# First block's gated unit by rows on centred x, its result turned by DMA

## Chip, cores, metric

One core of one Trainium2 chip. The metric is the device time of one execution in microseconds (us), lower is better. "The kernel before" and "the changed kernel" are the two versions compared.

## The reference, cut to what matters

```python
x = A_x                                   # (1, 2048, 640) bf16
xn = layernorm(x)                         # (x - mean) / sqrt(var + 1e-5), by rows
s = attention(xn, k_cache, v_cache, wq, wo)   # 32 heads, last 512 keys
g = silu((sigmoid(xn @ w_gate) * (xn @ w_up)) @ w_down)   # 640 -> 1536 -> 640
return x + s * g
```

The change is in `sigmoid(xn @ w_gate) * (xn @ w_up)` for the first 512 of the 2048 rows ("block 0"), at the start of the program. Since the layer norm's root is one number per row, `(xc * rstd) @ w = rstd * (xc @ w)` with `xc = x - mean`: with rows on the partitions the root can be applied after the matmul. "By rows" below means a result with the rows of x on the partitions and F along the free dimension, "by columns" one with F on the partitions; "turned" means transposed.

## The kernel before

Block 0, first four of twelve 128-column pieces of F, tile by tile of 128 rows, result with F on the partitions:

```python
def stats_end(t):                         # t < 2: root on ScalarE, reciprocal on VectorE
    nc.vector.bn_aggr(mv[:], ln[t][:])
    nc.scalar.activation(rstd[:], mv[:, 1:2], AF.Sqrt, bias=eps_t[:], scale=1.0)
    nc.vector.reciprocal(rstd[:], rstd[:])
    # (t >= 2: add on VectorE, pow -0.5 on GpSimd)

def normal(t, parts): ...                 # xn = (x - mean) * rstd, VectorE
def turn_pe(t, c0, c1, k): ...            # xn transposed on TensorE, copied to xnT[:, 0] by ScalarE

def tile_half(t, half, c0=0, c1=NCD):
    w = (wg_sb, wu_sb)[half]
    for c in range(c0, c1):
        for f in range(4):
            nc.tensor.matmul(bank[t % 3][:, half, f * P:(f + 1) * P],
                             lhsT=w[:, c, f * P:(f + 1) * P],
                             rhs=xnT[:, 0, c, t * P:(t + 1) * P], ...)   # 128 columns
# ... cut: sigmoid on ScalarE, product on VectorE, straight into hT[0]
for f in range(4, NF):                    # the other eight pieces: 512 columns
    gated(0, f, k, norm_piece(1, f - 4))  # norm_piece: layer norm of block 1, turned by DMA
for b in range(1, NB):
    for f in range(2):
        gated(b, f, k)
    for q in range(TQ):
        down(b - 1, q, k)                 # reads hT[b - 1]
    # ... cut
```

TensorE begins with 24 matmuls on dummy data ("dummies") while x is loaded.

The softmax here doesn't subtract the row's maximum and nothing guards it: scores larger than these inputs give would overflow.

## Time and profile before

| | before |
|---|---|
| time, median (range) of 4 runs | 922.59 us (922.28 to 923.13) |
| span of the profiled run | 920.3 us |
| TensorE busy | 915.1 us, 99% |
| first matmul of block 1 | 33.58 us |
| first down-projection | 37.89 us |

How to read it: TensorE is the bound, and its stream of matmuls runs without holes from about 9 us on, so whatever moves the start of a late matmul moves the end by as much. I use two such marks: the first matmul of block 1, which shows what the head cost, and the first down-projection, which is the first to read block 0's result. The profile's own lines are in the prediction.

### The profile page before, as it was taken

What the parts mean: (1) busy time and instruction counts of PE and PEld (TensorE: products, weight loads), DVE (VectorE), ACT (ScalarE), POOL (GpSimd) and SP (SyncE); (2) the same over time, 40 slices, a digit from 0 to 9 for tenths busy, and PEclk for the clock granted to TensorE, in tenths of its full rate; (3) what the DMA queues carried; (4) which work ended last, traced back from release to release, by engine and by line L of the source; (5) the groups of instructions that cost most, each with busy time, mean ns of one, the idle gap of its engine ahead of it and who ended that gap; (6) DMA issues with size and microseconds to landing.
All of it is one profiled execution on the core that took longest, in us unless ns stands there. A gap on an engine that the chain in (4) does not pass through costs nothing.

```text
span 920.3 us, 25202 instructions
## 1 busy us (share of the span) xinstructions
PE 915.1 (99%) x11460; PEld 628.5 (68%) x11460; DVE 491.7 (53%) x983; ACT 303.4 (33%) x336; POOL 133.6 (15%) x157
## 2 busy tenths in 40 slices
PE   9999999999999999999999999999999999999998
PEld 7445455466868686867676777777776767686875
DVE  5452522545646464645555555545564646464677
ACT  4222222255142424232333333242424151515150
POOL 1000100011002000200120011001100111065643
PEclk9999999999999999999999999999999999999999
DMA  9310330115434534342425162616251624263535
GB/s 320 81 30 1 89 86 1 43 62 88 78 63 106 86 57 83 93 99 42 98 81 111 36 104 79 113 28 112 65 109 43 116 61 94 63 113 111 90 81 136
DMA packets 163147, 77.14 MB, mean 84 GB/s; under 512 B 140992, under 2 KB 158608, under 8 KB 163040
## 3 DMA queue, kind: packets, MB, share of 16 engines
q1 hardware_dynamic: 155680, 53.62, 29.5%
q0 software_dynamic: 5808, 20.52, 7.9%
q8 instruction: 89, 1.46, 0.7%
q10 hardware_dynamic: 1552, 1.39, 0.5%
q14 instruction: 18, 0.15, 0.0%
HBM read 39.45 MB, written 2.62 MB: 46 GB/s over the span
## 4 chain that ended last, share of the span: by engine, by line
PE 99%; DVE 0%; ACT 0%; DVEq 0%; issue 0%
PE bank L504 22%; PE bank L433 21%; PE bank L455 19%; PE bank L415 18%; PE bank L242 10%; PE bank L254 6%; PE bank L381 1%; PE bank L287 1%; PE bank L190 0%; PE bank L539 0%; DVE o_sb L485 0%; DVE gate L490 0%; PE bank L226 0%; ACT xnT L228 0%; DVEq L641 0%
## 5 line engine op out<-in xcount | busy, mean ns | idle before, releaser
L419 ACT ACTIVATE E<-bank 128x1024 bf16<-128x1024 f32 x256 | 255.5, 1023 | 456.4 <-PE bank L415 456.3
L433 PE MATMUL bank<-xnT,wq_sb 64*128 64x512 bf16 x1800 | 226.4, 376 | 0.0
L504 PE MATMUL bank<-wo_sb,oT 64*128 64x320 bf16 x2688 | 205.2, 296 | 0.0
L415 PE MATMUL bank<-qT,kT 64*128 64x512 bf16 x1536 | 200.7, 376 | 0.0
L455 PE MATMUL bank<-vbuf,E 64*128 64x193 bf16 x4096 | 195.3, 243 | 0.0
L455 PEld LDWEIGHTS <-E 64*128 64x128 bf16 x4096 | 178.8, 94 | 10.2 <-issue 0.3
L504 PEld LDWEIGHTS <-oT 64*128 64x128 bf16 (+1 forms) x2892 | 163.2, 94 | 30.8 <-issue 0.5
L440 DVE CAST qT<-bank 128x1024 bf16<-128x1024 f32 x90 | 110.2, 1225 | 128.5 <-PE bank L433 128.5
L433 PEld LDWEIGHTS <-wq_sb 64*128 64x128 bf16 x1800 | 105.9, 100 | 87.2 <-issue 0.4
L415 PEld LDWEIGHTS <-kT 64*128 64x128 bf16 x1536 | 88.1, 94 | 73.5
L468 DVE TENSOR_TENSOR o_st<-bank,rden 128x768 bf16<-128x768 f32 x128 | 122.5, 957 | 4.4
L519 DVE TENSOR_TENSOR acc<-bank,acc 128x640 f32<-128x640 f32 x96 | 79.0, 823 | 20.2 <-PE bank L504 20.2
L118 POOL DMA_DIRECT2D vbuf<-in_A_v_cache_dram x28 | 21.1, 753 | 313.9 <-PE bank L455 310.9
L438 DVE COPY seen<-bank 128x2 f32<-128x2 f32 x90 | 14.3, 159 | 79.1 <-PE bank L433 79.1
L467 DVE RECIPROCAL rden<-bank 128x4 f32<-128x4 f32 x128 | 23.4, 183 | 60.6 <-PE bank L455 59.5
L242 PE MATMUL bank<-xnT,wg_sb 128*128 128x512 bf16 x220 | 54.7, 379 | 0.0
L242 PE MATMUL bank<-xnT,wu_sb 128*128 128x512 bf16 x220 | 54.7, 379 | 0.0
L248 DVE TENSOR_TENSOR hT<-bank,sig 128x512 bf16<-128x512 f32 x44 | 30.3, 689 | 42.1 <-ACT sig L245 42.1
L254 PE MATMUL bank<-wd_sb,hT 128*128 128x512 bf16 (+1 forms) x384 | 52.8, 299 | 0.0
L245 ACT ACTIVATE sig<-bank 128x512 bf16<-128x512 f32 x44 | 26.3, 597 | 68.4 <-PE bank L242 65.3
L254 PEld LDWEIGHTS <-hT 128*128 128x128 bf16 x384 | 29.7, 98 | 23.1
L242 PEld LDWEIGHTS <-wu_sb 128*128 128x128 bf16 x220 | 21.5, 98 | 26.0
(55 smaller groups left out, 367.5 us busy)
## 6 DMA issues: line engine op xcount, KB each, us to landing
wo_sb<-in_A_wo_dram SPq DMA_DIRECT2D x7, 960.0 KB, 5.5
wq_sb<-in_A_wq_dram POOLq DMA_DIRECT2D x7, 960.0 KB, 6.1
k_st<-in_A_k_cache_dram POOLq DMA_DIRECT2D x14, 384.0 KB, 5.3
vbuf<-in_A_v_cache_dram POOLq DMA_DIRECT2D x28, 192.0 KB, 3.4
row<-in_A_x_dram POOLq DMA_DIRECT2D x16, 160.0 KB, 3.1
oT<-o_st SPq DMA_TRANSPOSE x128, 3.5
x_sb<-in_A_x_dram SPq DMA_DIRECT2D x3, 640.0 KB, 10.8
wd_sb<-in_B_w_down_dram SPq DMA_DIRECT2D x1, 1920.0 KB, 14.3
```

What stands on the lines that cost most here:

```text
L242: nc.tensor.matmul(bank[k][:, half, 0:r1 - r0], lhsT=w[:, c, f * P:(f + 1) * P], rhs=xnT[:, b, c, r0:r1], start=(c == 0), stop=(c == NCD - 1))
L245: nc.scalar.activation(sig[:, 0:r1 - r0], bank[k][:, 0, 0:r1 - r0], AF.Sigmoid)
L248: nc.vector.tensor_tensor(hT[b][:, f, r0:r1], bank[k][:, 1, 0:r1 - r0], sig[:, 0:r1 - r0], ALU.mult)
L254: nc.tensor.matmul(wide(k)[:, d0:d1], lhsT=hT[b][:, f, q * P:(q + 1) * P], rhs=wd_sb[:, f, d0:d1], start=(f == 0), stop=(f == NF - 1))
L415: nc.tensor.matmul(bank[k][:, i, :], lhsT=kT[r, pr, j, c * P:(c + 1) * P], rhs=q[r, pr * DJ + j, :], start=(j == 0), stop=(j == DJ - 1))
L419: nc.scalar.activation(E[u, pr][:, c, :, :], bank[k][:], AF.Exp, scale=scale_qk)
L433: nc.tensor.matmul(bank[k][:, half, :], lhsT=wq[r, c, col:col + DJ * (P - 1) + 1:DJ], rhs=xnT[r, b, c, :], start=(c == 0 and not second), ...
L440: nc.vector.tensor_copy(qT[u][:, 2 * m:2 * m + 2, :], bank[k][:])
L455: nc.tensor.matmul(o4[:, q, 0:DH + 1], lhsT=e[r, c, h % 2, q * P:(q + 1) * P], rhs=vbuf[r, h, c, 0:DH + 1], start=(turn == 0 and qq == 0 a ...
L468: nc.vector.tensor_tensor(o_st[u][:, :, h * DH:(h + 1) * DH], o4[:, :, 0:DH], rden[:].to_broadcast([P, TQ, DH]), ALU.mult)
L504: nc.tensor.matmul(res[:, half, :], lhsT=oT[u][r, cc, q * P:(q + 1) * P], rhs=wo[r, cc, half * HD:(half + 1) * HD], start=(turn == 0 and c ...
L519: nc.vector.tensor_tensor(cols(acc[:, t, :]), res, cols(acc[:, t, :]), ALU.add)
```

## The change

Intent: take the root out of the chain that the first matmul waits for, and give block 0 matmuls of 512 columns throughout.

```diff
+        xcT = xnT[:, NB - 1, :, :]              # centred x lies in block 3's place for now
+        h_row = wB.tile([P, TQ, F], BF16, name="h_row")
...
+        def centred(t, parts=((0, 3 * P), (3 * P, D))):
+                nc.vector.tensor_scalar(xc[:, d0:d1], xt[t][:, d0:d1], ln[t][:, 0:1], None,
+                                        op0=ALU.subtract)
...
-                for f in range(FT):
-                    nc.tensor.matmul(bank[t % 3][:, half, f * P:(f + 1) * P],
-                                     lhsT=w[:, c, f * P:(f + 1) * P],
-                                     rhs=xnT[:, 0, c, t * P:(t + 1) * P],
+                nc.tensor.matmul(bank[k][:, half, :], lhsT=xcT[:, c, t * P:(t + 1) * P],
+                                 rhs=w[:, c, fg * FT:(fg + 1) * FT],      # FT = 512
...
+            nc.scalar.activation(sig[:], bank[k][:, 0, :], AF.Sigmoid, scale=rstd[:, 0:1])
+            if between is not None:
+                between()
+            nc.vector.scalar_tensor_tensor(h_row[:, t, fg * FT:(fg + 1) * FT], bank[k][:, 1, :],
+                                           rstd[:, 0:1], sig[:], ALU.mult, ALU.mult)
...
+        steps = [norm_piece(1, i) for i in range(TQ + 1)]
+        steps[TQ:] = [steps[TQ]] + [norm_first(t) for t in range(TQ)]   # xn of block 0, turned by DMA
+        for fg in range(1, F // FT):
+            for t in range(TQ):
+                tile_half(t, fg, k, 0)
+                tile_half(t, fg, k, 1)
+                tile_gated(t, fg, k, steps.pop(0) if steps else None)
+        hT[0] = hpool.tile([P, NF, TB], BF16, name="hT")
+        for t in range(TQ):
+            nc.sync.dma_start_transpose(hT[0][:, :, t * P:(t + 1) * P], h_row[:, t, :])
+        while steps:
+            steps.pop(0)()
```

(All roots now by pow on GpSimd; the table load for the square root goes.) The scaled x of block 0 is still needed, by the attention's queries, so it is normalised later (`norm_first`) and turned by DMA.

More of the change, by code (lines that the diff above doesn't have):

```diff
@@ L182 @@
         load_x(2 * TQ, TQ)
-        nc.scalar.activation(junk[:], eps_t[:], AF.Sqrt)
+        nc.scalar.activation(junk[:], eps_t[:], AF.Sigmoid)
         nc.gpsimd.memset(mhalf[:], -0.5)
@@ L198, in stats_half, with stats_aggr, stats_root, normal @@
             nc.vector.bn_stats(ln[t][:, i, :], xt[t][:, i * (D // 2):(i + 1) * (D // 2)])
-        def stats_end(t):
-            mv = bwork.tile([P, nc.vector.BN_AGGR_DIM], F32, name="mv")
-            rstd = bwork.tile([P, 1], F32, name="rstd")
+        def stats_aggr(t):
+            mv = bwork.tile([P, nc.vector.BN_AGGR_DIM], F32, name="mv0" if t < TQ else "mv")
             nc.vector.bn_aggr(mv[:], ln[t][:])
-            if t < 2:
-                nc.scalar.activation(rstd[:], mv[:, 1:2], AF.Sqrt, bias=eps_t[:], scale=1.0)
-                if t == 0:
-                    stats_half(1, 0)
-                nc.vector.reciprocal(rstd[:], rstd[:])
-            else:
-                nc.vector.tensor_scalar(rstd[:], mv[:, 1:2], eps, None, op0=ALU.add)
-                nc.gpsimd.tensor_tensor(rstd[:], rstd[:], mhalf[:], ALU.pow)
-            ln[t] = mv, rstd
-        def normal(t, parts=((0, D),)):
+            ln[t] = mv
+        def stats_root(t):
+            rstd = bwork.tile([P, 1], F32, name="rstd0" if t < TQ else "rstd")
+            nc.vector.tensor_scalar(rstd[:], ln[t][:, 1:2], eps, None, op0=ALU.add)
+            nc.gpsimd.tensor_tensor(rstd[:], rstd[:], mhalf[:], ALU.pow)
+            ln[t] = ln[t], rstd
+        def normal(t):
             mv, rstd = ln[t]
             xn = xpool.tile([P, D], BF16, name="xn")
+            nc.vector.tensor_scalar(xn[:], xt[t][:], mv[:, 0:1], rstd[:, 0:1],
+                                    op0=ALU.subtract, op1=ALU.mult)
+            xn_t[t] = xn
+        xn_t = {}
+        def centred(t, parts=((0, 3 * P), (3 * P, D))):
+            xc = xpool.tile([P, D], BF16, name="xn")
             for d0, d1 in parts:
-                nc.vector.tensor_scalar(xn[:, d0:d1], xt[t][:, d0:d1], mv[:, 0:1], rstd[:, 0:1],
-                                        op0=ALU.subtract, op1=ALU.mult)
-            ln[t] = xn
+                nc.vector.tensor_scalar(xc[:, d0:d1], xt[t][:, d0:d1], ln[t][:, 0:1], None,
+                                        op0=ALU.subtract)
+            xn_t[t] = xc
         def turn_pe(t, c0=0, c1=NCD, k=3):
@@ L225, in turn_pe @@
             for c in range(c0, c1):
-                nc.tensor.transpose(pT[:, c, :], ln[t][:, c * P:(c + 1) * P], ident[:])
+                nc.tensor.transpose(pT[:, c, :], xn_t[t][:, c * P:(c + 1) * P], ident[:])
             for d0, d1 in ((c0, c1),) if c1 - c0 < NCD else ((0, 3), (3, NCD)):
-                nc.scalar.activation(xnT[:, 0, d0:d1, t * P:(t + 1) * P], pT[:, d0:d1, :], AF.Copy)
+                nc.scalar.activation(xcT[:, d0:d1, t * P:(t + 1) * P], pT[:, d0:d1, :], AF.Copy)
         def turn_dma(t):
             q = t % TQ
-            nc.sync.dma_start_transpose(xnT[:, t // TQ, :, q * P:(q + 1) * P], ln[t][:])
+            nc.sync.dma_start_transpose(xnT[:, t // TQ, :, q * P:(q + 1) * P], xn_t[t][:])
         hT = {}
@@ L270, in step, with tile_half, tile_gated, norm_first @@
                     stats_half(t, 1)
-                    stats_end(t)
+                    stats_aggr(t)
+                    stats_root(t)
             return step if i <= TQ else None
-        FT = 4
-        hT[0] = hpool.tile([P, NF, TB], BF16, name="hT")
-        def tile_half(t, half, c0=0, c1=NCD):
+        FT = 4 * P
+        def tile_half(t, fg, k, half, c0=0, c1=NCD):
             w = (wg_sb, wu_sb)[half]
             for c in range(c0, c1):
-                for f in range(FT):
-                    nc.tensor.matmul(bank[t % 3][:, half, f * P:(f + 1) * P],
-                                     lhsT=w[:, c, f * P:(f + 1) * P],
-                                     rhs=xnT[:, 0, c, t * P:(t + 1) * P],
-                                     start=(c == 0 and f == 0), stop=(c == NCD - 1),
-                                     skip_group_check=True)
-        sigs = {}
-        def tile_sigmoid(t):
-            sigs[t] = bwork.tile([P, TB], BF16, name="sig")
-            nc.scalar.activation(sigs[t][:], bank[t % 3][:, 0, :], AF.Sigmoid)
-        def tile_gated(t):
-            nc.vector.tensor_tensor(
-                hT[0][:, 0:FT, t * P:(t + 1) * P],
-                bank[t % 3][:, 1, :].rearrange("p (f n) -> p f n", f=FT),
-                sigs[t][:].rearrange("p (f n) -> p f n", f=FT), ALU.mult)
+                nc.tensor.matmul(bank[k][:, half, :], lhsT=xcT[:, c, t * P:(t + 1) * P],
+                                 rhs=w[:, c, fg * FT:(fg + 1) * FT],
+                                 start=(c == 0), stop=(c == NCD - 1))
+        def tile_gated(t, fg, k, between=None):
+            rstd = ln[t][1]
+            sig = bwork.tile([P, TB], BF16, name="sig")
+            nc.scalar.activation(sig[:], bank[k][:, 0, :], AF.Sigmoid, scale=rstd[:, 0:1])
[3 more added lines that the diff above has]
+                                           rstd[:, 0:1], sig[:], ALU.mult, ALU.mult)
+        def norm_first(t):
+            def step():
+                normal(t)
+                turn_dma(t)
+            return step
         dummy(18)
@@ L308 @@
         stats_half(0, 1)
-        stats_end(0)
-        normal(0, ((0, P), (P, 3 * P), (3 * P, D)))
+        stats_aggr(0)
+        centred(0, ((0, P), (P, 3 * P), (3 * P, D)))
+        stats_half(1, 0)
+        stats_half(1, 1)
+        stats_aggr(1)
+        centred(1)
+        stats_root(0)
+        stats_root(1)
         turn_pe(0, 0, 1)
         turn_pe(0, 1, 3, 2)
-        tile_half(0, 0, 0, 1)
+        tile_half(0, 0, 0, 0, 0, 1)
         turn_pe(0, 3, NCD, 1)
-        tile_half(0, 0, 1)
@@ L317 @@
-        stats_half(1, 1)
-        stats_end(1)
-        normal(1, ((0, 3 * P), (3 * P, D)))
-        tile_half(0, 1, 0, 2)
+        tile_half(0, 0, 0, 0, 1)
         turn_pe(1, 0, 3)
-        tile_half(0, 1, 2, 3)
         turn_pe(1, 3, NCD, 2)
-        nc.scalar.activation(junk[:], eps_t[:], AF.Sigmoid)
-        tile_half(1, 0)
-        tile_half(0, 1, 3)
-        tile_sigmoid(0)
-        stats_half(2, 0)
-        stats_half(2, 1)
-        stats_end(2)
-        stats_half(3, 0)
-        stats_half(3, 1)
@@ L335 @@
-        normal(2)
-        stats_end(3)
-        tile_gated(0)
-        normal(3)
+        tile_half(0, 0, 0, 1, 0, 3)
+        tile_half(1, 0, 1, 0)
+        tile_half(0, 0, 0, 1, 3)
+        for t in (2, 3):
+            stats_half(t, 0)
+            stats_half(t, 1)
+            stats_aggr(t)
+            centred(t)
+            stats_root(t)
+        tile_gated(0, 0, 0)
         for t in range(1, TQ):
             if t > 1:
-                tile_half(t, 0)
-            tile_half(t, 1, 0, 1)
+                tile_half(t, 0, t % 3, 0)
+            tile_half(t, 0, t % 3, 1, 0, 1)
@@ L343 @@
             if t + 1 < TQ:
                 turn_pe(t + 1)
-            tile_half(t, 1, 1)
-            tile_sigmoid(t)
-            tile_gated(t)
+            tile_half(t, 0, t % 3, 1, 1)
+            tile_gated(t, 0, t % 3)
+        steps = [norm_piece(1, i) for i in range(TQ + 1)]
+        steps[TQ:] = [steps[TQ]] + [norm_first(t) for t in range(TQ)]
         k = 1
-        for f in range(FT, NF):
-            gated(0, f, k, norm_piece(1, f - FT))
-            k = (k + 1) % 4
+        for fg in range(1, F // FT):
[3 more added lines that the diff above has]
+                tile_gated(t, fg, k, steps.pop(0) if steps else None)
+                k = (k + 1) % 4
```

## The prediction

> **What bounds the kernel now.** I read four views of the kernel before, in this order: the page's summary, the chain that ended last over the first 50 us, the timeline of the first 17 us, and the DMA issues with the moving rate of a lone transpose. The summary and the shares of the chain:
>
> ```profile
> span 920.3 us, 25202 instructions
> PE 915.1 (99%) x11460; PEld 628.5 (68%) x11460; DVE 491.7 (53%) x983; ACT 303.4 (33%) x336; POOL 133.6 (15%) x157
> PE 99%; DVE 0%; ACT 0%; DVEq 0%; issue 0%
> ```
>
> TensorE is busy 915.1 of 920.3 us. Nothing that the change does on VectorE, ScalarE or the queues counts unless TensorE stands still for it, or is spared columns or a wait. So the question is small: which columns go, which TensorE waits go, and which come. The chain over the first 50 us says where TensorE now waits inside the region that the change touches:
>
> ```profile
> 1.06 4.21 PE bank L190 x24
> 5.27 0.22 PE bank L226
> 5.49 0.02 issue
> 5.51 0.29 ACT xnT L228
> ...
> 7.86 0.18 PE bank L226 x3
> 8.04 0.02 issue
> 8.07 0.50 ACT xnT L228
> 8.57 0.04 issue
> 8.61 1.95 PE bank L287 x32
> ```
>
> L190 is the warm-up with dummy matmuls, L226 the transposes of x on TensorE, L228 ScalarE's copy of them to SBUF, L287 the first block's 128-column matmuls. There are two holes: about 0.3 us at 5.5 us and 0.5 us at 8.1 us, both ended by a copy of transposed x. The second is there because tile 1 of x is normalised late. The timeline shows why:
>
> ```profile
> 4.10 0.21 DVE L203 BATCH_NORM_AGGREGATE mv<-st 128x2 f32<-128x12 f32 x1
> 4.23 0.44 DVE L198 BATCH_NORM_STATS2 st<-x_sb 128x6 f32<-128x320 bf16 x1
> 4.35 0.29 ACT L205 ACTIVATE rstd<-mv,eps_t 128x1 f32<-128x1 f32 x1 [1.18 <-DVE mv L203]
> 4.67 0.16 DVE L208 RECIPROCAL rstd<-rstd 128x1 f32<-128x1 f32 x1
> 4.87 0.82 DVE L218 TENSOR_SCALAR xn<-x_sb,mv,rstd 128x128 bf16<-128x128 bf16 x3
> ...
> 6.65 0.28 ACT L205 ACTIVATE rstd<-mv,eps_t 128x1 f32<-128x1 f32 x1
> 6.97 0.16 DVE L208 RECIPROCAL rstd<-rstd 128x1 f32<-128x1 f32 x1 [0.63 <-ACT rstd L205]
> 7.17 0.64 DVE L218 TENSOR_SCALAR xn<-x_sb,mv,rstd 128x384 bf16<-128x384 bf16 x2
> ```
>
> The root (ScalarE, then a reciprocal on VectorE) sits between the mean and the normalised x: 0.54 us in tile 0 (4.33 to 4.87), and in tile 1 0.63 us of idle plus the reciprocal. In the same timeline the first 512-column matmul of block 0 starts at 16.31 us, block 1 at 33.58, and the first down-projection of block 0 at 37.89.
>
> **What the Trainium skill says.** "TensorE: Matmul & The Clock Gate", section "Wait — 56ns, not 53.3ns?": a warm matmul of N columns starts N/2.4 GHz plus about 2.5 ns after the one before, 55.6 ns for 128 and 215.7 ns for 512. The trace agrees: twenty of 128 from 11.56 to 12.68 us are 56 ns each, five of 512 from 20.63 to 21.71 are 216 ns. So by rows costs the same per column. "ScalarE: Activation LUTs", section "What ACT_TABLE_LOAD costs": 1283 ns for the load, and about 93 ns more per pointer operand of an ACTIVATE; the trace has loads of 1283 ns, and tiny ACTIVATEs of 203 ns without and 290 ns with a pointer bias. "VectorE: DVE Perf Modes", section "Why PSUM operands drop a tier": an fp32 PSUM source runs at 1x, so I expect the new three-operand product to cost what the old one does, 690 ns for 512; no run shows the new one yet. "DMA: Bandwidth & Descriptors", section "Anatomy of one DMA", puts a fixed 2.0 us on a transfer (measured there on another issue path); here a lone transpose of 160 KB lands in 2.6 us, 1.8 of which is not movement (below).
>
> **The change part by part.**
>
> Matmuls. Removed: 160 of 128 columns (4 tiles x 2 weights x 5 chunks x 4). Added: 40 of 512. Saved: 40 x (4 x 55.6 - 215.7) ns = 0.27 us. The other 80 of block 0 are 512 wide before and after; the 20 transposes of x stay.
>
> Head of the chain. Centring needs only the mean. VectorE: aggregate of tile 0 ends at 4.31, so the three centred parts run 4.33 to 5.15 instead of 4.87 to 5.69. But the dummies occupy TensorE until about 5.14 (six of 64 columns issue by then), so of the 0.54 us only about 0.1 comes through. Then tile 1: two statistics 0.89 (to 6.05), aggregate 0.21 (6.27), two centred parts 0.38 + 0.34, done by 7.0 us where before it was 7.81. TensorE, walked through: transposes from 5.14, first copy to 5.68, matmul c0 at 5.71, c1 and c2 at 6.10, c3 and c4 at about 6.70 to 7.13; transposes of tile 1 to 7.41; three matmuls with the up weights to 8.06, which cover the copies of tile 1 (7.5 to 8.35); so the hole of 0.5 us at 8.1 closes. From there without waits: tile 1's gate 1.08 and tile 0's last two 0.43 to 9.57; tile 1's up with the transposes of tile 2 1.36; tile 2 with the transposes of tile 3 2.44; tile 3 2.16; the end is 15.53. Against 16.31: **0.78 us saved**, 0.27 of it per-matmul cost. The weights allow it: the up weights' halves were issued at 2.13 and 3.17 and land 4.9 and 5.1 us later (7.03, 8.27); they are used at 7.41 and 9.14. The second ScalarE table load (1.28 us at 8.85) goes, but no TensorE wait hung on it.
>
> Eight gated tiles of ten 512-column matmuls take 8 x 2.157 = 17.26 us as before: block 1 starts at 32.8 instead of 33.58. VectorE in that stretch is tied to the arrival of x at 19.41 and does the same statistics; x of block 1 was turned by a transpose issued near 29.0 us and in place by 31.6, still ahead of 32.8. Three of block 0's four normalisations (0.44 each) now lie in the last three tiles, where VectorE had only 0.69 us of product per 2.16 us.
>
> The turn of the result. Four transposes of 128x1536 (384 KB) are new, and stand on the same queue behind three new ones of 160 KB. The kernel before gives the cost of a transpose:
>
> ```profile
> xnT<-xn SPq DMA_TRANSPOSE x5, 2.6
> oT<-o_st SPq DMA_TRANSPOSE x128, 3.5
> L232 SPq DMA_TRANSPOSE xnT<-xn x12: 1200/1202/1411, 21.9 to 105.5; - x12
> L477 SPq DMA_TRANSPOSE oT<-o_st x128: 1209/1287/2633, 207.2 to 907.5; - x128
> ```
>
> The last number of the first two is issue to landing; the triple in the others is the queue's time for one in ns. The issue takes 1.2 to 1.3 us for 160 KB and for 192 KB alike, so I take 1.3 for 384 KB too. The lone one at 59.31 moves data at about 215 GB/s at its peak: 164 kB in 0.76 us, so 1.84 us is fixed; 393 kB then takes 1.83 us and lands about 3.7 us after its issue begins. When does it begin? Block 1's last transpose holds the queue until 30.2; the three new normalisations end at about 30.0, 31.2 and 32.3, their transposes hold it until 33.8; so the first turn of the result is issued at 33.8 and lands at **37.5**. TensorE, after two gated groups of block 1 (2 x 2.157 from 32.8), wants it at **37.1**: a new wait of about 0.4 us. The next lands 1.8 to 2 us later each, and a down-projection takes 3.26 us (37.89 to 50.93 for four), so only the first waits.
>
> Sum: 922.42 - 0.78 + 0.4 = **922.0 us**. All later stages shift with TensorE unchanged: block 0's scaled x in its usual place is wanted only by the queries after 163 us.
>
> **The rivals.** (1) The turn lands late. If the queue's time grows with size (2.6 us for twice the chunks), the first lands at about 39 and the wait is 1.9 us: 923.5. For it: the longest issue recorded is 2.63 us. Against: 160 and 192 KB cost the same, and longer ones have a wait inside. (2) The turn is hidden. If the three small transposes are issued earlier or the landing is nearer 3 us, only the head counts: 921.6. (3) The head gain doesn't come through: TensorE meets the next late thing, the weights or VectorE, which now has centring and roots of tiles 0 to 3. Then only the 0.27 us is saved and the wait shrinks with it: about 922.2. For it: DMA is saturated from 2 to 24 us (about 350 GB/s), and landings move a few tenths. (4) Fewer, larger matmuls make the block much faster: ruled out by the equal cost per column; even losing all of the stretch from 5.25 to 16.31 us would be 1.2%.
>
> **Range and chances.** The rivals span 921.6 to 923.5, and three runs of before spread 0.85 us. Range 920.9 to 923.5. 2% is 18 us, more than the whole stretch that is rewritten, so within 2% is nearly certain: faster 0.005, same 0.985, slower 0.01.
>
> **What would show it.** Right: L226 starts near 5.15, no hole near 8 us; block 0's second part starts near 15.5; the chain then shows one new piece of under 1.5 us before the first down-projection, put down to the transposes into hT; everything later is before's, shifted. The product from PSUM is about 690 ns, the sigmoid about 690 (597 plus a pointer). Wrong: a down-projection waiting several us, or each of the four waiting (the transposes are then slower than 3.26 us each); block 1's first matmul waiting for its x; a hole at 6 to 9 us put down to the weights; or the tail's length changing.

## The result, and the profile after

The changed kernel: 922.85 us median of 4 runs (922.62 to 923.09), against 922.59 of before; ratio 1.0002, 95% interval 0.9985 to 1.002. (Ratios are the mean time of one kernel's fast runs over that of the other's fast runs of the same rounds, so not quite the ratio of the medians.) Inside the predicted range, but the predicted sign (0.4 us down) did not come: if anything it is 0.3 us up. The range, 920.9 to 923.5, held both signs, so that the time fell inside it says little about the two terms of the sum. The profile says why, since in the trace a matmul's start can be compared to within hundredths of a microsecond.

Summary of the changed kernel:

```profile
span 920.8 us, 24985 instructions
PE 915.1 (99%) x11340; PEld 623.3 (68%) x11340; DVE 493.7 (54%) x989; ACT 302.3 (33%) x332; POOL 134.1 (15%) x159
```

The chain that ended last (the work that set the end, followed back from the last instruction to what released it) over the first 60 us of the changed kernel (start, us, what):

```profile
1.06 4.34 PE bank L194 x24
5.40 0.12 PE bank L235
5.52 0.02 issue
5.54 0.29 ACT xnT L237
5.83 0.05 issue
5.88 0.57 PE bank L293
...
13.04 18.14 PE bank L293 x84
31.19 0.02 issue
31.21 0.70 ACT sig L300
31.91 0.02 issue
31.93 0.75 DVE h_row L303
32.68 0.37 DVE xn L218
33.05 0.02 issue
33.07 1.20 SPq L241
34.27 0.05 issue
34.32 3.83 DMA hT<-h_row
38.15 0.05 issue
38.20 13.21 PE bank L263 x96
```

From 31.2 us the chain leaves TensorE: a sigmoid, a product, a late normalisation of block 0, its transpose on the queue (SPq is the queue of transfers that SyncE issues; L241), then the turn of the result, and only then the first down-projection (L263). The hole near 8 us is gone. What TensorE waited for in the changed kernel that it did not wait for before (total us, times, longest):

```profile
PE bank L263 <- DMA hT<-h_row: 0.5, 1, 0.5
```

One new wait, before the first of four down-projections. Its full size is better read from the starts: block 1's first matmul is at 33.17 us, its two groups take 4.32 us, so the down-projection could have started at 37.49 and started at 38.20: 0.71 us.

| mark | before | after | difference |
|---|---|---|---|
| first matmul of block 1 | 33.58 | 33.17 | -0.41 |
| first down-projection | 37.89 | 38.20 | +0.31 |
| 500th matmul from the end | 877.37 | 877.69 | +0.32 |
| last matmul | 916.25 | 916.76 | +0.51 |

So the head gained 0.41 us, the turn took back 0.72, and for 840 us nothing changed the shift. The last 0.19 arose at 878 to 883 us, among VectorE, GpSimd and the loads of x at the end, in code that the change does not touch; that stretch took 38.8 to 39.4 us over the profiles, 38.9 and 39.4 in two of the kernel before. I don't count it.

The head has a second thing in it. The first real matmul of 512 columns took 0.57 us here (at 5.88 in the chain above). The dummies show it: their group in the kernel before, then in the changed kernel (duration ns min/median/max, first and last start):

```profile
L190 PE MATMUL bank<-warm x24: 193/421/421, 1.1 to 5.1; 128*128 128x256 bf16 x18, 128*128 128x64 bf16 x6
```

```profile
L194 PE MATMUL bank<-warm x24: 242/421/421, 1.1 to 5.2; 128*128 128x256 bf16 x18, 128*128 128x64 bf16 x6
```

The same instructions on the same data; but the shortest 64-column dummies took 193 ns before and 242 after. In the first profile TensorE reached full speed before the dummies ended, in the second it had not. The trace's clock record puts the rise at 4.98 us and 6.27 us. The Trainium skill, "TensorE: Matmul & The Clock Gate", section "Part 1: The HAM clock gate", says the gate opens after about 3.4 us of activity, counted in a free-running window, so that the moment varies from run to run. The records here agree on the free-running part: in all twelve profiles of this study the granted clock changes only at moments that lie whole multiples of 3.413 us apart (268 of them, 914.77 us, from the rise to the fall at the end in this profile). In eleven of them the rise came 2.9 to 5.8 us after the first dummy (8 is the exception). So some of the missing head gain may be luck and not the change. The experiments test that as well.

### The profile page after: what moved, and what is told of

Its sections match the earlier page's. It is cut to its first block, busy times and chain, and to the rows that moved or that the text cites. A ratio compares the mean times of both kernels' runs of the same rounds, so it can differ in the third digit from the quotient of the medians.

```text
span 920.8 us, 24985 instructions
## 1 busy us (share of the span) xinstructions
PE 915.1 (99%) x11340; PEld 623.3 (68%) x11340; DVE 493.7 (54%) x989; ACT 302.3 (33%) x332; POOL 134.1 (15%) x159
## 4 chain that ended last, share of the span: by engine, by line
PE 98%; DVE 1%; DMA 0%; SPq 0%; ACT 0%; issue 0%; DVEq 0%
PE bank L518 22%; PE bank L447 21%; PE bank L469 19%; PE bank L429 18%; PE bank L251 8%; PE bank L263 6%; PE bank L293 3%; PE bank L395 1%; PE bank L194 0%; PE bank L553 0%; DMA hT<-h_row 0%; DVE gate L504 0%; DVE o_sb L499 0%; SPq L241 0%; PE bank L235 0%; DVE h_row L303 0%
## 5 line engine op out<-in xcount | busy, mean ns | idle before, releaser
L263 PE MATMUL bank<-wd_sb,hT 128*128 128x512 bf16 (+1 forms) x384 | 52.8, 299 | 0.5 <-DMA hT<-h_row 0.5
L263 PEld LDWEIGHTS <-hT 128*128 128x128 bf16 x384 | 29.6, 98 | 23.9 <-DMA hT<-h_row 1.0
L257 DVE TENSOR_TENSOR hT<-bank,sig 128x512 bf16<-128x512 f32 x36 | 24.8, 690 | 38.2 <-ACT sig L254 38.2
L251 PE MATMUL bank<-xnT,wg_sb 128*128 128x512 bf16 x180 | 44.7, 379 | 0.0
L251 PE MATMUL bank<-xnT,wu_sb 128*128 128x512 bf16 x180 | 44.7, 379 | 0.0
L254 ACT ACTIVATE sig<-bank 128x512 bf16<-128x512 f32 x36 | 21.5, 597 | 55.8 <-PE bank L251 52.7
L97 POOL DMA_DIRECT2D wq_sb<-in_A_wq_dram x7 | 6.3, 900 | 210.5 <-PE bank L447 210.5
```

Source lines behind the costliest of these rows:

```text
L251: nc.tensor.matmul(bank[k][:, half, 0:r1 - r0], lhsT=w[:, c, f * P:(f + 1) * P], rhs=xnT[:, b, c, r0:r1], start=(c == 0), stop=(c == NCD - 1))
L257: nc.vector.tensor_tensor(hT[b][:, f, r0:r1], bank[k][:, 1, 0:r1 - r0], sig[:, 0:r1 - r0], ALU.mult)
L263: nc.tensor.matmul(wide(k)[:, d0:d1], lhsT=hT[b][:, f, q * P:(q + 1) * P], rhs=wd_sb[:, f, d0:d1], start=(f == 0), stop=(f == NF - 1))
```

## The experiments

Theory: the head gains 0.4 us in the profiled run, and would have gained about 0.4 us more had TensorE been at full speed as early as in the profile of before; the turn is issued too late and gives 0.7 us or more back. Rivals: the new wait is only the visible one of several; the turn is not on the path; centring is worth nothing; the change itself made TensorE slow to warm.

All outputs are right. Times of the kernel before: 922.71 us median for the first four, 922.35 for the next four, 922.53 for the last two.

**1. The turn as soon as it can go.** Each tile's rows are turned right after its last product; the late normalisations come after.

```diff
-                tile_gated(t, fg, k, steps.pop(0) if steps else None)
+                tile_gated(t, fg, k, steps.pop(0) if len(steps) > TQ else None)
+                if fg == F // FT - 1:
+                    turn_h(t)          # hT[0] <- h_row[:, t, :] by DMA transpose
```

> Each tile's rows are turned by DMA as soon as its last product is written, and the four late normalisations of block 0 come after. Theory (the head gains 0.4 us, the late turn gives 0.7 us back): the first down-projection finds its hT landed, no wait before it; it starts 4.3 us after block 1's first matmul instead of 5.0, and the time is 0.7 us below the changed kernel, about 922.1. Rival (the wait is only moved: a turn lands when the queue can take it, or another transpose of block 1 then comes late): a wait of 0.3 us or more stays somewhere between 32 and 52 us, and the time stays near 922.8.

921.61 us median of 5 (921.48 to 922.34); ratio to before 0.999, interval 0.9977 to 1.0002. The chain:

```profile
12.87 20.29 PE bank L293 x94
33.16 4.32 PE bank L251 x20
37.47 13.04 PE bank L263 x96
```

It never leaves TensorE: the down-projections follow block 1's two groups without a wait, at 37.31 us (the chain gives the end of the overlap). The list of waits has no hT in it, and no other wait took its place. Against the changed kernel's profile the first down-projection is 0.89 us earlier: 0.71 for the wait, 0.18 from the head (clock rise at 5.67 us instead of 6.27). The profiled executions differ by 1.14 us (922.62 and 921.48), more than the 0.7 expected: the other 0.25 us arose in the stretch at the end, which I don't count. The wait theory holds, the "only moved" rival falls.

**2. The turn later still.** All four late normalisations and their transposes before the turn.

```diff
+        while steps:
+            steps.pop(0)()
         hT[0] = hpool.tile(...)
         for t in range(TQ):
             nc.sync.dma_start_transpose(hT[0][:, :, t * P:(t + 1) * P], h_row[:, t, :])
-        while steps:
-            steps.pop(0)()
```

> All four late normalisations and their transposes go ahead of the turn. Theory (the turn is on the path that sets the end, and its start is set by the normalisation and the transpose ahead of it on the queue): one more transpose (1.2 us) and one more normalisation behind the last product move the first turn from 34.3 to about 36.4 us, the wait before the first down-projection grows from 0.7 to about 2.8 us, and the time by 2.1 us to 924.9. Rival (something else sets the first down-projection): the time stays within 0.5 us of the changed kernel.

925.97 us median of 5, in two kinds: 924.20 and 924.41 with a mean clock of 1.000, and 925.97 to 926.25 with 0.998. The chain of the profiled run, of the faster kind:

```profile
34.42 0.45 DVE xn L218
34.87 0.02 issue
34.89 1.20 SPq L241
36.09 0.05 issue
36.14 3.80 DMA hT<-h_row
39.94 0.05 issue
39.98 12.07 PE bank L263 x87
```

The turn is issued at 36.14 (expected 36.4), lands after 3.80 us, and the wait is 2.83 us (39.98 less 32.83 + 4.32), 2.1 more than in the changed kernel, as expected. The profiled execution is 1.79 us above that of the changed kernel (924.41 and 922.62), not 2.1, because it had a faster head: block 1 began at 32.83 us, 0.34 earlier, with the clock's rise at 4.96. The slower kind, 1.8 us more, was not expected; experiments 7 and 9 go after it.

**3. By rows, but on normalised x.** The root is back in the head; no scale in the sigmoid or product, no second normalisation; turned early as in 1.

```diff
-        centred(0, ((0, P), (P, 3 * P), (3 * P, D)))
+        root_act(0)                                        # Sqrt on ScalarE, reciprocal
+        normal(0, ((0, P), (P, 3 * P), (3 * P, D)))
-            nc.scalar.activation(sig[:], bank[k][:, 0, :], AF.Sigmoid, scale=rstd[:, 0:1])
+            nc.scalar.activation(sig[:], bank[k][:, 0, :], AF.Sigmoid)
-            nc.vector.scalar_tensor_tensor(..., rstd[:, 0:1], sig[:], ALU.mult, ALU.mult)
+            nc.vector.tensor_tensor(..., sig[:], ALU.mult)
```

> By rows and turned by DMA (early, as in e1_turn_early), but on x normalised before it is transposed, as in the kernel before: square root and reciprocal back in the head, no scale in the sigmoid or the product, no second normalisation. Theory (centring is worth the hole near 8 us): the hole of about 0.5 us is back, the first matmul of the second part of block 0 starts at about 16.1 us for a TensorE that is warm by 5 us (16.31 before; 15.90 changed, cold until 6.1), no wait before the down-projection, time about 922.4. Rival (centring is worth nothing, by rows everything): it starts at 15.6 to 15.9, and the time equals that of e1_turn_early.

922.68 us median of 4 (922.48 to 922.95), the kernel before's time. That is 1.07 us above experiment 1 (921.61; 921.48 to 922.34), which differs from it by the centring alone, with what belongs to it; the ranges don't overlap. So the rival that centring is worth nothing falls by the times. Block 1 began at 33.74, the hole near 8 us was back (0.47 us from one start to the next at 8.5), and there was no wait for hT. But TensorE was cold until 6.89 us in this profile (the second part of block 0 began at 16.47, where 16.1 was expected of a warm one), so how much is centring and how much the clock isn't separated by it alone; see 10.

**4. The kernel before, once more.**

> The kernel before, unchanged, for one more profile. Theory (the moment at which TensorE reaches full speed varies from execution to execution, and took about 0.4 us of the head's gain in the profiled run of the changed kernel): this profile, and those of the three other kernels of this call, show the change from 213 ns per dummy matmul to full speed at scattered times, some over 0.5 us from the 4.95 us of the first profile. Rival (the change made TensorE warm later): this profile has it at 4.95 us again and all three others at about 6.1 us.

One execution, 923.37 us. Its dummies:

```profile
L190 PE MATMUL bank<-warm x24: 242/421/421, 1.1 to 5.2; 128*128 128x256 bf16 x18, 128*128 128x64 bf16 x6
```

242 ns, as in the changed kernel's profile: the clock rose at 6.12 us. With 1 to 3 (5.67, 4.96, 6.89) the rise is scattered over two microseconds with no regard to the kernel. The rival falls: the change did not make TensorE warm later. This profile shows another accident too: a wait of 0.4 us on the up weights' transfer. Together they put block 1's first matmul at 34.35 us, 0.77 after the first profile of the very same kernel. That is as much as the change could win.

**5. Two dummies less** (on top of 1).

```diff
-        dummy(18)
+        dummy(16)
```

> e1_turn_early with two of the eighteen wide dummy matmuls less (0.43 us of cold TensorE). Theory (with centred x the dummies, not x, hold the first transpose; after that copies of ScalarE bound the head): the first transpose moves from 5.2 to about 4.8 us, the second part of block 0 starts 0.2 to 0.4 us before that of e1_turn_early at the same warm-up moment, time about 921.3. Rival (the weights' landings bind then): the first transpose is earlier, but a wait on the weights' transfers takes its place and the second part starts where it did; or TensorE is cold for longer and nothing is gained.

921.48 us median of 5 (921.12 to 921.84), 0.999 of before (0.9978 to 1.0003); 1 had 0.999 too. The first transpose moved from 5.21 to 4.79; block 1 began at 32.85 with the clock's rise at 6.08, where 1 had 32.99 with 5.67. So some 0.15 us or more is gained in the trace, but the two times don't separate them. Inconclusive in the time, and not the rival's picture: no wait on weights came.

**6. The changed kernel once more.**

> The changed kernel as it is, for one more profile and in the same rounds as e5_fewer_dummies. Theory (two parts of opposite sign): again a wait of 0.9 to 1.2 us between the last matmul of block 1's second group and the first down-projection (0.92 in its first profile, larger when the head was faster), the time 922.6 to 923.1 as before, the second part of block 0 starting at 15.5 to 15.6 us if TensorE is warm by 5 us, later by up to 0.5 us if not. Rival: the wait was an accident of one execution and is gone.

922.96 us median of 5 (921.91 to 923.41). Block 1 began at 33.13 (clock's rise at 5.53), the first down-projection at 38.71: a wait of 1.26 us, larger than in the first profile. (The expectation counted from the start of the last matmul, 0.92 then; so counted it is 1.48 here, over the 0.9 to 1.2 expected.) The chain has it:

```profile
34.80 0.05 issue
34.85 3.82 DMA hT<-h_row
38.67 0.05 issue
38.71 2.35 PE bank L263 x16
```

The turn was issued 0.53 us later than in the first profile. Here block 1's x reached VectorE at 20.16 us instead of 18.19, so the last four of the seven small transposes of x stood back to back on the queue (29.63, 30.93, 32.25, 33.57) and the turn behind them, as the prediction had pictured it. The wait is no accident; between these two profiles its size went with the arrival of x.

**7. Experiment 2 once more**, for a profile of the slower kind.

> e2_turn_late as it is, for a profile of its slower kind (three of five executions were at 926.0 to 926.3 us with a mean clock of 0.998, two at 924.2 to 924.4 with 1.000). Theory (TensorE, idle for some 3 us, is slowed for a while afterwards, and that is the other 1.7 us): if the execution is of the slower kind, matmuls after the wait at 37 to 40 us run at half rate (432 ns for 512 columns) for about 3.4 us. Rival: the loss lies elsewhere in the program. If it is of the faster kind, nothing is learnt.

924.39 us: the faster kind again, block 1 at 32.79, down-projection at 39.97, wait 2.86 us. It repeats 2 and teaches nothing on the other kind.

**8. Experiment 3 once more.**

> e3_rows_scaled as it is, for one more profile of its head. Theory (centring saves about 0.5 us in the head): second part of block 0 starts at about 16.1 us if TensorE is warm by 5 us, up to 16.6 if not; in either case 0.4 us or more after a centred kernel of the same warm-up moment. Rival: it starts at 15.5 to 15.7 in a warm execution.

924.64 us, spoilt: no matmul started from 5.57 to 6.73 us (0.8 us of it idle), for the gate weights' transfer, while TensorE was still cold, and it reached full speed only at 10.49 us; block 1 began at 35.73.

**9. A standstill of eight microseconds.** Experiment 2 with block 0's four small transposes issued twice.

```diff
         while steps:
             steps.pop(0)()
+        for t in range(TQ):
+            turn_dma(t)
```

> e2_turn_late with the four transposes of block 0's normalised x issued a second time (same data) ahead of the turn, so that TensorE stands still longer before the first down-projection. Theory (the wait counts one to one, and a standstill of some 3 us or more can leave TensorE at half speed for some 3.4 us, which was the other 1.7 us of e2_turn_late's slower executions): the turn is issued 4.8 us later, at about 41 us, the wait grows from 2.9 to about 7.7 us, and in every execution TensorE is slow for a while after it: 922.9 + 7.0 + 1.7 = about 931.5 us, and the matmuls after the wait show half rate (432 ns for 512 columns). Rival (the slower executions of e2_turn_late had another cause): full rate right after the wait, and about 929 us.

932.3 us median of 4 (932.09 to 932.66), ratio to before 1.0108 (1.0091 to 1.0125); expected 931.5, the rival's 929. The wait was 8.19 us (32.99 + 4.32 to 45.51). By stretches of time (stretch, its length in us; busy time of PE, PEld, DVE, ACT and POOL; then PEclk, the granted clock, the DMA share and GB/s; a stretch is left out after the first line):

```profile
36.00:37.00 1.00, 1.00 (x6) 0.49 (x5) 0.67 (x1) 0.00 (x0) 0.00 (x0) 1.00 0.81 154
...
39.00:40.00 1.00, 0.00 (x0) 0.00 (x0) 0.00 (x0) 0.00 (x0) 0.00 (x0) 0.82 0.76 146
40.00:45.00 5.00, 0.00 (x0) 0.00 (x0) 0.00 (x0) 0.00 (x0) 0.00 (x0) 0.50 0.83 156
45.00:49.00 4.00, 3.49 (x13) 1.66 (x14) 0.00 (x0) 0.00 (x0) 0.00 (x0) 0.50 1.14 211
49.00:50.00 1.00, 0.95 (x4) 0.51 (x4) 0.00 (x0) 0.00 (x0) 0.00 (x0) 0.56 1.15 209
50.00:52.00 2.00, 1.97 (x16) 1.14 (x16) 0.16 (x1) 0.70 (x1) 0.00 (x0) 1.00 0.87 201
```

The clock fell to a half at 39.6 us, 2.3 us after the last matmul had ended, and rose at 49.9, 4.4 us after work had started again. The four down-projections took 15.2 us from first start to the next group instead of 13.0. So a long wait costs its length and then some 2 us more. For the slower kind of experiment 2 this fits: a wait of 2.8 us can outlast the 2.3 us seen here, and its mean clock was 0.2% lower, which is 1.8 us of the span. It need not, since the clock changes only at its steps of 3.413 us: in the profiles of 2 and 7 one such step fell 1.9 us after the last matmul had ended and the clock stayed up, and the next came only after work had started again. One step at half clock would cost half of 3.413, 1.7 us, as the two kinds differ by (an estimate). But no profile of the slower kind was caught, so there it stays inferred.

**10. Experiment 3 a third time.**

> e3_rows_scaled once more, since the second profile was spoilt by late weights. Theory (centring saves some 0.4 us in the head at the same warm-up moment): TensorE at full speed by 5 us: second part of block 0 at about 16.0 us; at 6 us: about 16.2. Rival: within 0.15 us of the centred kernels (15.56 for a warm-up at 4.95 us, 15.73 at 5.67, 15.90 at 6.27).

922.14 us. The clock had risen by 3.95 us, so TensorE was warm for all real work, as in 2 and in the first profile of before. Block 1 began at 33.28, the second part of block 0 at 16.02, as expected. This gives a ladder of three profiles, all warm before the first transpose. The first matmuls of block 0's second part, in the order of the table:

```profile
16.31 1.24 PE L242 MATMUL bank<-xnT,wg_sb 128*128 128x512 bf16 x5
```

```profile
16.02 1.24 PE L302 MATMUL bank<-wg_sb,xnT 128*128 128x512 bf16 x5
```

```profile
15.57 1.24 PE L293 MATMUL bank<-wg_sb,xnT 128*128 128x512 bf16 x5
```

| form | clock rise | block 1's first matmul | step |
|---|---|---|---|
| by columns, normalised (before) | 4.98 | 33.58 | |
| by rows, normalised (10) | 3.95 | 33.28 | -0.30 |
| by rows, centred (2) | 4.96 | 32.83 | -0.45 |

Each of the first two rows is one profile; the third was repeated (7: 32.79). In the first two the first transpose waited for x, whose statistics began at 3.18 and 3.11 us. With that 0.07 us taken out the steps are nearer 0.23 and 0.52; their sum stands. The difference of 1.07 us between the times of 3 and 1 is larger than the step of centring here; the rise of the clock in the executions without a profile may be in it.

## Why the prediction was right or wrong

**TensorE as the bound, and equal cost per column: right.** Busy time is 915.1 us in both. The matmul term was put at 0.27 us; the step by rows alone is 0.30 in the ladder, 0.23 with the arrival of x taken out.

**The head: right for a warm TensorE, wrong in the profiled run.** Predicted 0.78 us; the ladder gives 0.75, of which centring has 0.45, and the hole near 8 us closed as said. The changed kernel's own profile shows 0.41. The step that failed there is the walk "transposes from 5.14, first copy to 5.68, matmul c0 at 5.71, c1 and c2 at 6.10": it took for granted that TensorE is warm at 5.1 us, since the one profile of before showed it so. In the run it was cold until 6.27; c0 took 0.57 us and held the transposes behind it back (c3 started at 7.03 instead of 6.70). The kernel before suffers the same in other executions (4), so this is scatter on both sides, not a cost of the change. In the six profiles with this head and all the dummies block 1's first matmul went with the rise of the clock: 32.79 us for a rise at 4.92, 32.83 for 4.96, 32.99 for 5.51, 33.13 for 5.53, 32.99 for 5.67 and 33.17 for 6.27. That the one profile of before had an early moment and that of the changed kernel a late one is chance. The working also gave the three centred parts of tile 0 the old 0.82 us (to 5.15); they took 0.64 (4.35 to 4.99), which counted for nothing, since the dummies held the first transpose until 5.21.

**The turn: right in kind, too small.** Predicted wait 0.4 us; measured 0.71 and 1.26. Landing took 3.83 us where 3.7 was said. The larger part is the issue: said 33.8, measured 34.32. The failing step is "the three new normalisations end at about 30.0, 31.2 and 32.3". They ended at 28.73, 30.88 and 33.04:

```profile
30.44 0.44 DVE L218 TENSOR_SCALAR xn<-x_sb,mv,rstd 128x640 bf16<-128x640 bf16 x1
31.01 1.24 PE L293 MATMUL bank<-wg_sb,xnT 128*128 128x512 bf16 x5
31.21 0.69 ACT L300 ACTIVATE sig<-bank,rstd 128x512 bf16<-128x512 f32 x1 [1.47 <-PE bank L293]
31.93 0.75 DVE L303 SCALAR_TENSOR_TENSOR h_row<-bank,rstd,sig 128x512 bf16<-128x512 f32 x1 [1.05 <-ACT sig L300]
...
32.60 0.44 DVE L218 TENSOR_SCALAR xn<-x_sb,mv,rstd 128x640 bf16<-128x640 bf16 x1
```

The first is early because x of block 1 reached VectorE at 18.19 us in this profile and not at 19.41. The last one stands behind the product of the tile before it, and that behind a sigmoid which starts only after the tile's last matmul, of the up half (sigmoid 31.21, product 31.93, normalisation 32.60; the up half ended at 31.18), although the gate half that it reads was done a microsecond earlier. The timeline of before shows the same (gate half 29.26 to 30.34, up half to 31.42, sigmoid at 31.62), and the working ignored it. "I take 1.3 for 384 KB too" was off as well: the queue took 1.50 to 1.87 us for each turn,

```profile
L363 SPq DMA_TRANSPOSE hT<-h_row x4: 1497/1766/1874, 34.3 to 39.5; - x4
...
DMA to landing us min/median/max: 3.8/4.6/5.7
```

but only the first had to be on time, and it was the shortest, so this cost little. "Only the first waits" was right.

**The sum.** 0.78 against 0.4 was to give -0.4; it gave -0.41 + 0.72 = +0.31 at the first down-projection. For the wait, 0.71 us lies nearer to rival (2), hidden, and the 1.26 of experiment 6 nearer to rival (1), 1.9 us. The reason of (1), a queue time that grows with size, is true in part (1.20 to 1.50 us for the first turn), but the issue came 0.52 us later than forecast, and the landing took only 0.13 us longer. Rival (3), the head gain not coming through, happened in part, by the clock and not by weights.

**Small costs.** The sigmoid with a pointer scale takes 687 ns (about 690 predicted); the three-operand product 750 ns instead of the 690 expected:

```profile
L303 DVE SCALAR_TENSOR_TENSOR h_row<-bank,rstd,sig x12: 741/750/751, 10.9 to 34.1; 128x512 bf16<-128x512 f32 x12
```

Its 60 ns lie once on the path to the turn.

**A better version.** With the turn early (1, or 5 with two dummies less) the head's gain survives: 921.6 and 921.5 us against 922.4 to 922.7 of before, 0.1%. Both intervals of the ratio just include 1, so by the ratio it isn't settled, although in both each of the five runs was below each of the nine of before; the chain without a wait is what shows where the gain comes from.

## What to carry to other kernels

When a change moves work off the path and adds a transfer of its result, write down when the transfer can be issued, not only how long it takes: here a queue order that put transposes first that were not needed until much later turned a gain into nothing, and moving the turn ahead of them gave it back. Compare heads only at the same warm-up moment of TensorE: take two profiles of the unchanged kernel before trusting tenths of a microsecond from one. And a standstill of TensorE can cost more than its length: one of 8.2 us cost about two more, and one of 2.8 us sometimes some 1.7 more, which was not traced.

## What the Trainium skill lacked or had wrong

- "TensorE: Matmul & The Clock Gate", section "Part 1: The HAM clock gate": it gives a scatter of the warm-up moment of 500 ns either way. Here it rose at 3.95 to 6.89 us in eleven profiles with nearly the same dummies, just under one step of 3.413 us, and at 10.49 in the one where TensorE was idle for 0.8 us while cold.
- The same section has the clock fall after an idle window of about 3.4 us. Here it fell 2.3 us after the last matmul (9), and at the ends of the twelve profiles about 2.5 to 5 us after it.
- "DMA: Bandwidth & Descriptors", section "Anatomy of one DMA": the fixed 2.0 us is given for another issue path only; a transpose within SBUF came near it, about 1.84 us (an estimate from its 2.6 us for 160 KB at 215 GB/s), and 384 KB landed in 3.83 us. No page gives, for trn2 by name, the queue's own time for issuing a transpose: 1.20 us for 160 KB and 1.50 to 1.87 for 384 KB.
- "VectorE: DVE Perf Modes", section "The perf-mode tier table (the rule you actually need)" has no row for the product of a tensor, a pointer scalar and a tensor: 750 ns for 512 fp32 columns from PSUM, where the product of two tensors takes 690.
